# Two more products of a blocked matmul by an inner Strassen level, with one operand's block sums kept in DRAM

## The chip, the cores and the metric

The kernel runs on one core of a Trainium2 chip. The metric is the device time of one execution in microseconds (us): the median of nine runs, and beside it one execution taken by the hardware profiler, from which all durations come. TensorE (PE) multiplies, VectorE (DVE) and ScalarE (ACT) do elementwise work, GpSimd (POOL) small things, and SyncE (SP) issues nearly all DMAs from one queue.[...]

## The reference

```
x: 1 x 2048 x 1024 (bf16), w1: 1024 x 3584, b1: 3584, w2: 3584 x 1024, b2: 1024
y = (x - mean) / sqrt(var + 1e-5)          # per row of 1024
h = gelu(y @ w1 + b1)                      # tanh form
out = h @ w2 + b2
```

Matmul 1 is `y @ w1` with its bias and gelu, matmul 2 is `h @ w2 + b2`.

## The kernel before, in words

The 2048 rows are cut into two blocks of 1024 (`s` = 0 and 1). Each block runs matmul 1 and then matmul 2.

**Strassen (Winograd's form).** Each matmul of a block is split into 2 x 2 quarters and made of seven products in place of eight. A product multiplies a quarter or a sum of quarters (S1 to S4 on the side of the rows, T1 to T4 on the side of the weights), and the seven results are added up in PSUM and SBUF. In matmul 1 (`mm1_unit`, L579) this runs over seven chunks of w1 per block (numbered 0 to 6 in block 0 and 7 to 13 in block 1), two units in each; only chunk 0 is plain (`mm1_plain`). A unit is P1, P5, P6, P2, P7, P3, P4 (`SEQ1`), each four matmuls of 512 columns at L604, and the two units of a chunk alternate. ACT takes snapshots of PSUM (L617), DVE adds (L622, four per chunk) and ACT applies gelu (L628), which writes h in four quarters h11, h12, h21, h22, each of 14 slices of 128. DVE also forms T1 to T4 of each w1 chunk (L537).

**Matmul 2** (`mm2_block`, L746) has the order 5, 1, 2, 6, 7, 3, 4 (`SEQ2`). Products 5, 6 and 7 are plain (`plain`, L788): four tiles of 14 matmuls, 128 x 512, at L792. Products 1, 2, 3 and 4 (`INNER`) use a second, inner Strassen level (`inner`, L806): seven sub-products in the order of `SEQ1`, each 14 matmuls of 256 columns at L838. DVE forms the inner sums of both operands for each (four of h and four of w2, 128 x 1792, at L679): those of h into t1 buffers, those of w2 into old w1 buffers, and for the last product into others. Results are added up by ACT copies (L776) and DVE additions (L756), and stored from `o_sb` by SP (L785).

**The w2 operands.** Block 0's matmul 1 forms the outer sums T1 to T4 of w2 (`w2_prep`, L698) and writes them to DRAM (`w2_sums`). `load_w2` (L734) brings a whole quarter, raw or summed, 1792 KB in one DMA, into one of the homes A and B (`w2a_sb`), C (in `yw_sb`) and H (in `h_sb`). Block 1 loads seven such quarters.

**What sets the order.** Nothing is ordered by hand. Each operation is recorded with its dependencies, a cost and a due time, and a list planner (`Planner.place`, L127) fixes each engine's order and gives out PSUM banks and buffers. DMAs have a planned rate and a fixed time there. The program then has waits on semaphores in front of an instruction where its inputs come from another engine or a DMA; `war` lists name what must have finished before a buffer is written again. `done(p)` is the list of all users of product p, and `h_war` makes the gelus of the next block wait for the readers of a quarter of h.

**Block border.** While block 0's products 3 and 4 end, SP loads w1 for chunks 7 and 9 (chunk 8 is loaded long before), and T1 and B11 for block 1; the first units of block 1's matmul 1 are interleaved with product 4.

Of the kernel before, what the change touches and what calls it, by code (L numbers as in the profile page):

```python
# [6 lines left out]
ALU = mybir.AluOpType  # L7
BF16 = mybir.dt.bfloat16
# [23 lines left out]
SEQ2 = (5, 1, 2, 6, 7, 3, 4)  # L32
INNER = ((1, 2, 3, 4), (1, 2, 3, 4))
# [203 lines left out]
def bass_standalone__mixer_channel_mlp__prompt_kernel(  # L237
# [24 lines left out]
    with ExitStack() as es:  # L262
# [13 lines left out]
        e0_sb = sb("e0_sb", [P, HT // 2], F32)  # L276
        b1r_sb = sb("b1r_sb", [FT, P], BF16)
# [18 lines left out]
        NQ = NU * HT  # L296

# [6 lines left out]
        YN = KH * HT  # L304
        yop = {n: yw16[:, k * YN:(k + 1) * YN].rearrange("p (k n) -> p k n", n=HT)
# [357 lines left out]
        KI = NU // 2  # L663
        HI = HT // 2
# [29 lines left out]
        tq_ok = {r: [] for r in range(4)}  # L694
        x_gate = {}
# [50 lines left out]
        def mm2_block(s, W):  # L746
# [3 lines left out]
            for p in SEQ2:  # L750
                pt[p] = t0
                t0 += 7 * SUB if p in inn else TH * SLOT2
            A = {q: (h[q], [[h_ok[(s, q, u)]] for u in range(NU)]) for q in h}
            users = {p: [] for p in SEQ2}
# [26 lines left out]
            def store(q, t, n, ho, deps, at):  # L781
                r = (s * NT + (q // 10 - 1) * TH + t) * P
                c = (q % 10 - 1) * HT
                dst = of[r:r + n * P, c:c + HT].rearrange("(v p) c -> p v c", p=P)
                add("SP", 0.42, lambda e: e.dma_start(dst, o_sb[:, ho.k:ho.k + n, :]), deps, at + 0.5,  # L785
                    f"st{q}_{s}_{t}", sem=ho, inc=16, nbytes=n * P * HT * 2, frees=(ho,))
# [18 lines left out]

            def inner(p, a, b, xb, yb, war, O=None, bias=None, out=None, gate=()):  # L806

# [5 lines left out]
                Y = {f"{i + 1}{j + 1}": (b[0][:, i * KI:(i + 1) * KI, j * HI:(j + 1) * HI], b[1][i * KI:(i + 1) * KI])  # L813
                     for i in range(2) for j in range(2)}
                at = {r: pt[p] + k * SUB for k, r in enumerate(SEQ1)}

                def tt(dst, x, y, op, r, n):
                    return sums(dst, x, y, op, war.get((n[0], r), ()), at[r] - 3 * SUB, f"i{n}{r}_{nm}", step=KI)

                s1 = tt(xb[0], X["21"], X["22"], ALU.add, 5, "S")  # L820
                t1 = tt(yb[0], Y["12"], Y["11"], ALU.subtract, 5, "T")
                s2 = tt(xb[1], s1, X["11"], ALU.subtract, 6, "S")
                t2 = tt(yb[1], Y["22"], t1, ALU.subtract, 6, "T")
                s3 = tt(xb[2], X["11"], X["21"], ALU.subtract, 7, "S")
                t3 = tt(yb[2], Y["22"], Y["12"], ALU.subtract, 7, "T")
                s4 = tt(xb[3], X["12"], s2, ALU.subtract, 3, "S")
                t4 = tt(yb[3], Y["21"], t2, ALU.subtract, 4, "T")
                opn = {1: (X["11"], Y["11"]), 2: (X["12"], Y["21"]), 3: (s4, Y["22"]), 4: (X["22"], t4), 5: (s1, t1),
                       6: (s2, t2), 7: (s3, t3)}
# [23 lines left out]
                if O is None:  # L853
                    g = Holder(snaps, 4)
                    f1 = copy(lambda: bank_q(c2), lambda: bank_q(c0), (subs[1],), end(1), f"f1_{nm}", alloc=c2)
                    k5 = copy(lambda: quart(g, 1, 1), lambda: bank_q(c5), (subs[5],), end(5), f"k5_{nm}", alloc=g)
                    sub(6, (f1,))
                    k2 = copy(lambda: quart(g, 0, 1), lambda: bank_q(c0), (subs[6], k5), end(6), f"k2_{nm}")
                    sub(2, (f1,))
                    r11 = copy(lambda: quart(g, 0, 0), lambda: bank_q(c2), (subs[2], k5), end(2), f"r11_{nm}", frees=(c2,))  # L860
                    sub(7, (k2,))
                    r22 = dve(lambda e: plus(e, quart(g, 1, 1), bank_q(c0), quart(g, 1, 1)), (subs[7], k5), end(7),
                              f"r22_{nm}")
                    sub(3, (k5,))
                    r12 = dve(lambda e: plus(e, quart(g, 0, 1), bank_q(c5), quart(g, 0, 1)), (subs[3], k2), end(3),
                              f"r12_{nm}", frees=(c5,))
                    sub(4, (r22,))
                    r21 = copy(lambda: quart(g, 1, 0), lambda: bank_q(c0), (subs[4], k5), end(4), f"r21_{nm}", frees=(c0,))
                    users[p] += list(subs.values()) + flat(s1, s2, s3, s4, t1, t2, t3, t4)
                    return g, {11: r11, 12: r12, 21: r21, 22: r22}, subs  # L870

                g, ok = O
                ho = [Holder(outs, 2), Holder(outs, 2)]
                kk = Holder(snaps)

                def o_q(i, j):
                    return o_sb[:, ho[i].k:ho[i].k + 2, j * HI:(j + 1) * HI]

                sd = copy(lambda: bank_q(c2), lambda: quart(g, 0, 0), (ok[11], subs[1]), at[1], f"s2_{nm}", alloc=c2)
                k1 = copy(lambda: sn_sb[:, kk.k, :], lambda: ps[:, c0.k, :], (subs[1],), end(1), f"k1_{nm}", alloc=kk)  # L880
# [4 lines left out]
                o11 = dve(lambda e: plus(e, o_q(0, 0), bank_q(c2),  # L885
                                         sn_sb[:, kk.k, :].rearrange("p (v c) -> p v c", v=2)), (subs[2], k1), end(2),
                          f"o11_{nm}", alloc=ho[0], frees=(c2, kk))
# [6 lines left out]
                store(out, 0, 2, ho[0], (o11, o12), end(3))  # L894
                sub(4, (o22,))
                o21 = dve(lambda e: plus(e, o_q(1, 0), bank_q(c0), quart(g, 1, 0)), (subs[4], ok[21], o12, o22), end(4),
                          f"o21_{nm}", frees=(c0, g))
                store(out, 2, 2, ho[1], (o22, o21), end(4))
                users[p] += list(subs.values()) + flat(s1, s2, s3, s4, t1, t2, t3, t4)
# [13 lines left out]
            def war_of(subs):  # L913
                return {(c, r): [subs[r]] for c in "ST" for r in subs}

            B = dict(W)

# [12 lines left out]
            g1, ok1, sub1 = inner(1, A[11], B[1], X0, Y0, war0, gate=(M5[2],), bias=(  # L930
# [10 lines left out]
            sub2 = inner(2, A[12], B[2], X0, Y0, war_of(sub1), O=(g1, okw), out=11)  # L941
# [25 lines left out]
            sub3 = inner(3, S4, B[3], X0, Y0, war_of(sub2), O=(g12, {11: O12[1], 12: O12[1], 21: O12[3], 22: O12[3]}), out=12)  # L967
            for m in (n - 2, n):
                w1_use[m] = w1_use[m] + done(3)
            for m in (n - 1, n):  # L970
                for k in range(1, 5):
                    t1_use[m][k] = t1_use[m].get(k, []) + done(3)

            end_b = s + 1 == NSB
            xe = x16.rearrange("p i d -> p (i d)") if end_b else h_flat[21]
            inner(4, A[22], B[4], halves(xe), halves(w2a16[:, 1].rearrange("p k n -> p (k n)")),
                  {(c, r): [o for i in range(NT) for o in x_free[(s, i)]] if end_b and c == "S" else done(7)
                   for c in "ST" for r in range(1, 8)},
                  O=(g3, {11: O3[1], 12: O3[1], 21: O3[3], 22: O3[3]}), out=21)
# [3 lines left out]
            return {"A": done(3), "B": done(4), "C": done(2), "ring": ring}  # L983

        tile_prio = [-100 + 2.3 * i for i in range(NT)]
        for i in range(NT):
# [6 lines left out]
            else:  # L993
# [6 lines left out]
        bias_ok = add("DVE", 0.4, lambda e: e.tensor_tensor(out=e0_sb[:, :], in0=b2_sb[:, HI:HT], in1=b2_sb[:, 0:HI],  # L1000
                                                            op=ALU.subtract), (b2_ld, dl_), 60.1, "e0")
# [4 lines left out]
        for s in range(NSB):  # L1006
            last = []
            for c in range(NC):
                n = s * NC + c
                t0 = base1[s] + c * 14 * SLOT  # L1010
                if n:
                    T = w1_sums(s, c, t0 - 2 * SLOT)
                    for v in range(2):
                        last += mm1_unit(s, c, v, T, t0 + v * SLOT)
                m = n + N_W1
                if m < (s + 1) * NC:
                    load_w1(s, m % NC, t0 + 14 * SLOT)
                if s == 0 and c == 1:
                    gate = (w1_use[0][-1],)
                    t11 = load_w2(0, "B", "B11", gate, t0 + 0.1)  # L1020
                    t1q = w2_prep(t11[1][0][0], gate, t0 + 8, 8.5)
            if s == 0:
                W = {5: t1q, 1: t11}
            else:
                W = {5: load_w2(s, "A", "T1", wfree["A"], base1[s] + 0.3 * T_MM1),
                     1: load_w2(s, "B", "B11", wfree["B"], base1[s] + 0.3 * T_MM1 + 0.1)}
            W["C"] = last
            wfree = wf = mm2_block(s, W)
            if s + 1 < NSB:
                for c in range(N_W1):  # L1030
                    load_w1(s + 1, c, base2[s] + 40 + c)
                for i in range(NT):
                    load_x(s + 1, i, [*x_gate[i]], base2[s] - 4 + i)
                    ln_act2(s + 1, i, base2[s] + 10 + 5 * i, wf["ring"])
                    dma_T(s + 1, i, base2[s] + 30 + 3 * i, ((*last, *(wf["C"] if i >= TH else ())), last))
                y_sums(s + 1, base1[s + 1] - 14, wf["C"])
# [59 lines left out]
```

## Time and profile before

| | us |
|---|---|
| median of nine runs (lowest, highest) | 347.89 (346.82, 348.80) |
| profiled execution: device time, span | 347.71, 346.0 |
| head: 0 to 29.73 | PE busy 25.57 |
| matmul 1, block 0: 29.73 to 99.66 | PE 69.93, DVE 58.23, ACT 48.13, DMA 318 GB/s |
| matmul 2, block 0: 99.66 to 183.90 | PE 84.24, DVE 69.92, ACT 46.80, DMA 205 GB/s |
| matmul 1, block 1: 183.90 to 263.42 | PE 79.52, DVE 45.04, ACT 54.88, DMA 80 GB/s |
| matmul 2, block 1: 263.42 to 342.48 | PE 79.05, DVE 60.70, ACT 15.99, DMA 137 GB/s |
| tail: 342.48 to 346.00 | DVE 0.69, then the last store |

The granted TensorE clock is full in every slice. The whole run moves 63.01 MB by DMA. In the profile a row of a chain gives start, length and what ran; a row of an engine's timeline gives start, length, the instruction, and in brackets the idle time before it and what ended it. Matmul rows carry a length that includes the drain of the pipeline (a 256-column matmul has 273 ns there), so lengths per matmul are taken from the chain: stretch divided by count. SP's rows are issues; the time from issue to landing stands apart (10.6 us for the T1 load at the border, 3.8 to 6.8 for w1 halves).

### The profile page before, as it was taken

Reading aid. Unit: us, or ns where it says so; the run is one execution under the profiler, and the core shown is the slowest. Engines: PE = TensorE matmul, PEld = TensorE weight load, DVE = VectorE, ACT = ScalarE, POOL = GpSimd, SP = SyncE. Lnnn points to the kernel's source line nnn. Section 1 sums busy time; section 2 is a strip of 40 time slices with the busy share of each in tenths; the row PEclk is TensorE's granted clock in tenths of the full one; section 3 lists DMA queues with packets and bytes.
Section 4 is the critical chain, followed back from the end, with each engine's and each line's share of the span. In section 5 each row is a group of like instructions: output and inputs, shape, how many; then the busy total and the mean of one; then the engine's idle time right before and its main releaser. Section 6 shows DMA issues by size and latency. Waiting matters only on the chain.

```text
span 346.0 us, 5462 instructions
## 1 busy us (share of the span) xinstructions
PE 338.3 (98%) x2179; PEld 202.5 (59%) x2179; DVE 255.1 (74%) x356; ACT 183.5 (53%) x303; POOL 23.5 (7%) x47
## 2 busy tenths in 40 slices
PE   5999999999999999999999999999999999999995
PEld 4976444444444886448865444444444587644885
DVE  4679988989566698959999565465329779796943
ACT  4774766766788878622115767666676324002110
POOL 2320000000003223410000000000000000000000
PEclk9999999999999999999999999999999999999999
DMA  7649999988964792595398531230004256029111
GB/s 254 234 93 290 353 344 341 293 294 280 371 221 134 243 243 47 124 333 197 105 390 254 164 123 45 77 123 0 0 0 148 83 198 213 32 72 392 53 63 61
DMA packets 54339, 63.01 MB, mean 182 GB/s; under 512 B 12970, under 2 KB 47786, under 8 KB 53418
## 3 DMA queue, kind: packets, MB, share of 16 engines
q1 hardware_dynamic: 54170, 62.54, 55.9%
q8 instruction: 17, 0.28, 0.3%
q10 hardware_dynamic: 144, 0.13, 0.2%
q14 instruction: 8, 0.07, 0.1%
HBM read 48.50 MB, written 11.53 MB: 174 GB/s over the span
## 4 chain that ended last, share of the span: by engine, by line
PE 97%; DMA 1%; DVE 1%; ACT 0%; POOL 0%; issue 0%
PE ps L604 45%; PE ps L838 25%; PE ps L792 21%; PE ps L562 5%; PE ps L468 1%; DMA x_sb<-in_x_dram 1%; DVE st_sb L391 0%; DVE o_sb L756 0%; ACT yw_sb L475 0%; POOL rstd_sb L398 0%; DVE x_sb L401 0%; DVE mv_sb L394 0%; DVE vpe_sb L395 0%; PE ps L379 0%
## 5 line engine op out<-in xcount | busy, mean ns | idle before, releaser
L604 PE MATMUL ps<-yw_sb,t_sb 128*128 128x512 f16 x416 | 96.2, 379 | 0.0
L792 PE MATMUL ps<-w2a_sb,h_sb 128*128 128x512 f16 x336 | 73.8, 379 | 0.0
L604 PE MATMUL ps<-yw_sb,w_sb 128*128 128x512 f16 x312 | 73.7, 379 | 0.0
L604 PEld LDWEIGHTS ps<-yw_sb,t_sb 128*128 128x128 f16 x416 | 40.5, 98 | 48.9 <-ACT h_sb L628 0.4
L792 PEld LDWEIGHTS ps<-w2a_sb,h_sb 128*128 128x128 f16 x336 | 32.9, 98 | 38.3
L622 DVE TENSOR_TENSOR sn_sb<-ps,sn_sb 128x512 f32<-128x512 f32 x54 | 36.5, 687 | 25.5 <-PE ps L604 25.5
L604 PEld LDWEIGHTS ps<-yw_sb,w_sb 128*128 128x128 bf16 x312 | 30.3, 98 | 36.3 <-ACT ps L617 0.6
L628 ACT ACTIVATE h_sb<-sn_sb,b_sb 128x512 f16<-128x512 f32 x54 | 38.6, 719 | 19.1 <-DVE sn_sb L622 16.6
L776 ACT COPY sn_sb<-ps 128x512 f32<-128x512 f32 x30 | 17.2, 581 | 45.4 <-DVE o_sb L756 33.4
L679 DVE TENSOR_TENSOR h_sb<-h_sb 128x1024 f16<-128x1024 f16 (+2 forms) x42 | 38.5, 948 | 2.1 <-ACT h_sb L628 2.1
L628 ACT ACTIVATE h_sb<-ps,b_sb 128x512 f16<-128x512 f32 x50 | 34.1, 684 | 8.8 <-PE ps L604 7.9
L617 ACT COPY sn_sb<-ps 128x512 f32<-128x512 f32 x49 | 28.7, 586 | 16.0 <-PE ps L604 15.8
L756 DVE TENSOR_TENSOR o_sb<-ps,sn_sb 128x512 bf16<-128x512 f32 x32 | 21.7, 687 | 14.9 <-PE ps L838 10.9
L838 PE MATMUL ps<-w_sb,t_sb 128*128 128x256 f16 x252 | 30.1, 273 | 0.0
L838 PEld LDWEIGHTS ps<-w_sb,t_sb 128*128 128x128 f16 x252 | 24.7, 98 | 3.1
L537 DVE TENSOR_TENSOR t_sb<-w_sb,t_sb 128x1024 f16<-128x1024 bf16 x26 | 17.9, 687 | 8.3 <-PE ps L604 7.2
L838 PE MATMUL ps<-w2a_sb,h_sb 128*128 128x256 bf16 (+1 forms) x182 | 21.8, 273 | 0.0
L537 DVE TENSOR_TENSOR t_sb<-w_sb 128x1024 f16<-128x1024 bf16 x26 | 17.7, 681 | 5.2 <-PE ps L604 4.1
L776 ACT COPY ps<-sn_sb 128x512 f32<-128x512 f32 x14 | 8.1, 589 | 24.4 <-PE ps L838 20.6
L679 DVE TENSOR_TENSOR t_sb<-h_sb 128x1792 f16<-128x1792 f16 x12 | 13.0, 1085 | 9.6 <-PE ps L838 9.5
L838 PEld LDWEIGHTS ps<-w2a_sb,h_sb 128*128 128x128 f16 x182 | 17.8, 98 | 3.1
L756 DVE TENSOR_TENSOR sn_sb<-ps,sn_sb 128x512 f32<-128x512 f32 x24 | 16.4, 684 | 4.1 <-PE ps L838 2.6
(82 smaller groups left out, 321.5 us busy)
## 6 DMA issues: line engine op xcount, KB each, us to landing
w_sb<-in_w_dram SPq DMA_DIRECT2D x28, 512.0 KB, 5.4
w2a_sb<-w_sums SPq DMA_DIRECT2D x5, 1792.0 KB, 7.4
w2a_sb<-in_w_dram SPq DMA_DIRECT2D x4, 1792.0 KB, 7.4
x_sb<-in_w_dram SPq DMA_DIRECT2D x21, 256.0 KB, 4.6
w_sums<-x_sb SPq DMA_DIRECT2D x21, 256.0 KB, 4.9
x_sb<-in_x_dram SPq DMA_DIRECT2D x15, 256.0 KB, 5.4
yw_sb<-in_w_dram SPq DMA_DIRECT2D x2, 1792.0 KB, 7.5
h_sb<-w_sums SPq DMA_DIRECT2D x2, 1792.0 KB, 11.0
```

The source lines that it names most:

```text
L468: fn = [(lambda e, j=j, k=k, hold=hold: e.transpose(out=ps16[:, hold.k, j * P:(j + 1) * P], in_=x16[:, i, k * HT + j * P:k * HT + (j + 1) ...
L537: return add("DVE", 0.65, lambda e: e.tensor_tensor(out=tv(k), in0=x0, in1=x1, op=ALU.subtract), [*deps, *war.get(k, ())], prio + 0.5 * k, ...
L562: fn = [(lambda e, b=b, hb=hold[f], f=f, k=k, t=t: e.matmul(ps[:, hb.k, t * P:(t + 1) * P], lhsT=lhs[:, k, f * P:(f + 1) * P], rhs=yop[f"A ...
L604: fn = [(lambda e, k=k: e.matmul(ps[:, hold[p].k, :], lhsT=lhs[:, k, :], rhs=yop[yo][:, k, :], start=(first and k == 0), stop=(k == KH - 1 ...
L617: return e.copy(out=dst, in_=src) if o_.eng == "ACT" else e.tensor_copy(dst, src)
L622: return add("DVE", 0.69, lambda e: e.tensor_tensor(out=sn_sb[:, hold_s.k, :], in0=ps[:, hold[p].k, :], in1=sn_sb[:, hold_s.k, :], op=ALU. ...
L628: r = h_ok[(s, q, u)] = add("ACT", 0.70, lambda e: e.activation(out=h[q][:, u, :], in_=src(), func=ACT.Gelu_apprx_tanh, bias=b1_sb[:, f:f ...
L679: o = add("DVE", cost2(w * dst.shape[-1]), lambda e, k0=k0, k1=k1: e.tensor_tensor(out=dst[:, k0:k1, :], in0=a[0][:, k0:k1, :], in1=b[0][: ...
L756: plus = lambda e, out, x, y: e.tensor_tensor(out=out, in0=x, in1=y, op=ALU.add)
L776: return act(lambda e: e.copy(out=out(), in_=src()), deps, at, name, **k)
L792: fn = [(lambda e, k=k, t=t: e.matmul(ps[:, banks_[t].k, :], lhsT=a[0][:, k, t * P:(t + 1) * P], rhs=b[0][:, k, :], start=(first and k == ...
L838: fn = [(lambda e, k=k, j=j: e.matmul(ps[:, bank[r].k, j * HI:(j + 1) * HI], lhsT=x[0][:, k, j * P:(j + 1) * P], rhs=y[0][:, k, :], start= ...
```

## The change

In block 1, six of the seven products of matmul 2 are inner ones, only product 6 stays plain, and product 1 comes first. The w2 operands of an inner product come as seven separate blocks of 448 KB, four of them inner sums from a new DRAM tensor, three of them blocks of a quarter, in rows of 512 bytes. The inner sums of products 1 to 4 are the ones that block 0 forms anyway; it now also stores them. Those of T1 and T3, which products 5 and 7 need, are formed by DVE during matmul 1 of block 1, in buffers of x and of the outputs. Block 0's computation and order are kept otherwise. New waits: block 0's inner sums and everything that counts as done with a product also wait for the stores. The planner makes all orders anew.

The order of TensorE's instructions is the same up to the end of matmul 1 of block 1. In SP's new order, around the border, stand: a store of product 4's T2 sum, the four w1 halves, four blocks, an output store, the stores of product 4's T3 and T4 sums, two output stores, four blocks (after a wait for product 4's stores), the load of T1 for its inner sums (after a wait for all outputs of block 0), w1 loads, four stores of inner sums, the load of T3. On ACT, the first gelu of block 1 waits for product 4's inner stores and stands behind four snapshots. On DVE, the first inner sum of T1 stands between the second and third addition of chunk 8, and that of T3 behind the sum of h that follows chunk 9.

```diff
-SEQ2 = (5, 1, 2, 6, 7, 3, 4)
-INNER = ((1, 2, 3, 4), (1, 2, 3, 4))
+SEQ2 = ((5, 1, 2, 6, 7, 3, 4), (1, 5, 2, 6, 7, 3, 4))
+INNER = ((1, 2, 3, 4), (1, 5, 2, 7, 3, 4))
...
+        ti = nc.dram_tensor("w2_inner_sums", [7, 4, P, KI, HI], FP16, kind="Internal").ap()
...
+            def inner_sums(p, b, yb, war):
...
+                def tt(n, x, y, r):
+                    res = sums(yb[n - 1], x, y, ALU.subtract, war.get(("T", r), ()), at[r] - 3 * SUB, f"iT{r}_{nm}", step=KI)
+                    if s + 1 < NSB:
+                        st = dma(ti[p - 1, n - 1], yb[n - 1], res[1][0], at[r] + 1, f"is{p}_{n}", f"is{n}",
+                                 P * KI * HI * 2)
+                        ti_ok[(p, n)] = [st]
+                        users[p].append(st)
+                        ti_st.setdefault(p, {})[r] = st
+                    return res
...
-            def inner(p, a, b, xb, yb, war, O=None, bias=None, out=None, gate=()):
+            def inner(p, a, Yo, xb, war, O=None, bias=None, out=None, gate=(), kk=None):
...
+            def last_block():
...
+                def fetch(p, names, prio):
+                    res = {}
+                    for k, (r, b) in enumerate(zip(SEQ1, names)):
+                        d = blk[b]
+                        if r > 3:
+                            j = {5: 1, 6: 2, 7: 3, 4: 4}[r]
+                            o = dma(d, ti[p - 1, j - 1], [*use[b], *ti_ok[(p, j)]], prio + 0.1 * k, f"wi{p}_{r}",
+                                    f"wi{b}", P * KI * HI * 2)
+                        else:
...
+                            o = dma(d, src, [*use[b], *dep], prio + 0.1 * k, f"wi{p}_{r}", f"wi{b}", P * KI * HI * 2)
+                        res[r] = (d, [[o]] * KI)
+                    return res
...
+                hold = {1: ("A0", "A1", "A2", "A3", "B0", "B1", "B2"), 5: ("V0", "V1", "Y0", "Y1", "Y2", "Y3", "Y4"),
+                        2: ("W0", "W1", "Y5", "Y6", "Y7", "X0", "X1"), 7: ("B0", "B1", "B2", "B3", "V0", "V1", "Y0"),
+                        3: ("Y1", "Y2", "Y3", "Y4", "W0", "W1", "Y5"), 4: ("Y6", "Y7", "X0", "X1", "A0", "A1", "A2")}
+                Yo = {1: fetch(1, hold[1], base1[s] + 0.5 * T_MM1), 5: fetch(5, hold[5], pt[1] - 10),
+                      2: fetch(2, hold[2], pt[1])}
...
+                g1, ok1, sub1 = inner(1, A[11], Yo[1], XX, warE, gate=(jobs[-3],), bias=(
+                    b2_sb[:, None, 0:HI].to_broadcast([P, 2, HI]), e0_sb[:, None, :].to_broadcast([P, 2, HI])))
...
+                g5, ok5, sub5 = inner(5, S1, Yo[5], XT, warX, gate=(sub1[6],), bias=(
+                    dl_sb[:, None, 0:HI].to_broadcast([P, 2, HI]), e1_sb[:, None, :].to_broadcast([P, 2, HI])))
+                give(hold[5], sub5)
+                B6 = load_w2(s, "A", "T2", [o for k in range(4) for o in use[f"A{k}"]], pt[5])
...
+                    V.append(copy(lambda t=t: tile_of(gv, t), lambda t=t: bank_t(hb[t]), (M6[t], *V[:1]), at, f"V_{s}_{t}",
+                                  alloc=gv if t == 0 else None))
...
+                gw, okq, sub7 = inner(7, S3, Yo[7], XT, war_of(sub5), O=(gv, okv), kk=dl_sb[:, :], gate=(sub5[5],))
...
+                        f.append(dve(lambda e, i=i, j=j, ho=ho: plus(
+                            e, o_sb[:, ho.k:ho.k + 2, j * HI:(j + 1) * HI], quart(gw, i, j), quart(g5, i, j)),
...
+        def t_inner(p, j, gate, prio):
+            x4 = x16.rearrange("p i d -> p (i d)")[:, 0:NQ].rearrange("p (k n) -> p k n", n=HT)
+            ld = dma(x4, tq[j], [*gate, *tq_ok[j]], prio, f"tl{p}", "tl", NU * P * HT * 2)
...
+            a1, s1 = tt(1, ob[0], Y[0, 1], Y[0, 0], (ld, *gate))
+            a3, s3 = tt(3, ob[1], Y[1, 1], Y[0, 1], (ld, *gate))
+            a2, s2 = tt(2, Y[1, 1], Y[1, 1], ob[0], (a1, a3))
+            a4, s4 = tt(4, Y[1, 0], Y[1, 0], Y[1, 1], (a2,))
+            return [s1, s2, s3, s4, a4]
...
-                W = {5: load_w2(s, "A", "T1", wfree["A"], base1[s] + 0.3 * T_MM1),
-                     1: load_w2(s, "B", "B11", wfree["B"], base1[s] + 0.3 * T_MM1 + 0.1)}
+                x_end = [o for i in range(NT) for o in x_free[(s, i)]] + wfree["outs"]
+                e5 = t_inner(5, 0, x_end, base1[s] + 0.15 * T_MM1)
+                e7 = t_inner(7, 2, e5, base1[s] + 0.4 * T_MM1)
+                W = {"A": wfree["A"], "B": wfree["B"], "x": e7, "C": last}
```

## The prediction

> **What bounds the kernel now.** I read the busy rows first, then the chain that ended last, then busy time by stretch, then the queues at the one border that the change disturbs. The profile's busy rows and its shares of the chain:
>
> ```profile
> PE 338.3 (98%) x2179; PEld 202.5 (59%) x2179; DVE 255.1 (74%) x356; ACT 183.5 (53%) x303; POOL 23.5 (7%) x47
> PE 97%; DMA 1%; DVE 1%; ACT 0%; POOL 0%; issue 0%
> ```
>
> TensorE is busy 98% of the span, and the chain runs through it almost alone. The chain in order of time (start, length, what) has no gap from 29.73 us on; of block 1 it reads:
>
> ```profile
> 183.90 79.52 PE ps L604 x368
> 263.42 12.09 PE ps L792 x56
> 275.50 16.81 PE ps L838 x154
> ...
> 302.94 18.13 PE ps L792 x84
> 321.07 21.41 PE ps L838 x196
> 342.48 0.02 issue
> 342.50 0.69 DVE o_sb L756
> ```
>
> Each piece starts where the last one ends. So a matmul taken out anywhere in block 1 shortens the run by its own length, as long as no new wait replaces it; and a faster or slower DVE, ACT or queue changes nothing until TensorE waits for it. Two rows of busy time by stretch (length; PE, PEld, DVE, ACT, POOL; clock; DMA share; GB/s), an inner stretch and matmul 1 of block 1:
>
> ```profile
> 275.51:292.31 16.80, 16.80 (x155) 15.01 (x154) 13.22 (x15) 6.62 (x12) 0.00 (x0) 1.00 0.61 216
> 183.90:263.42 79.52, 79.52 (x369) 35.83 (x368) 45.04 (x68) 54.88 (x87) 0.00 (x0) 1.00 0.26 80
> ```
>
> The clock is full in both. Weight loads fill 15.01 of 16.80 us in the inner stretch and still hide. In matmul 1 of block 1 the DMA engines are three quarters idle and DVE has 34 us free: the room that the change means to use.
>
> **The change part by part.**
>
> *Products 5 and 7 of block 1 go inner.* From the chain, 56 matmuls of 512 columns take 12.09 us (215.9 ns each) and 154 of 256 columns 16.81 us (109.2 ns each). A plain product is 56 of the first, an inner one 7 x 14 = 98 of the second: 10.70 us. Two products: 2 x (12.09 - 10.70) = **2.78 us** off TensorE. The Trainium skill (TensorE: Matmul & The Clock Gate, "The mechanism") speaks against this: it says a weight load overlaps a running matmul only when it goes to another row group. Every load here is 128x128, so 98 ns would then stand bare before each matmul: inner 98 x (98 + 109) = 20.3 us against plain 56 x (98 + 216) = 17.6, and the change would lose 5.4. The stretch above refutes it for this kernel (15.01 us of loads inside 16.80 us of matmuls): I take the row.
>
> *Removed in block 1:* 16 sums of w2 blocks on DVE (1.08 us each, products 1 to 4). *Added on DVE:* 8 sums of h for products 5 and 7 and 8 w2 sums inside matmul 1, so none net; some 8 more additions of 512 (0.69 us) in the results of 5 and 7, about 5.5 us, in a block where DVE is busy 60.7 of 79.06 us. The four sums of two SBUF operands have no row; I take the 0.69 us of the additions from PSUM. The last of them frees the buffer that ACT's copy for product 3 takes at 320.4; it ends at 319.7, at twice the cost at 320.4. Cost nil while DVE stays within one sub-product (1.53 us) of TensorE, as it does now, and no gain either, since TensorE waits for neither today; each lost us would count in full. ACT gets four copies in product 6 and loses as many elsewhere; it has 16.0 us of work in 79.
>
> *Start of block 1.* It now begins with an inner product, whose second sub-product needs a sum over all of h11. The last gelu of h11 runs at 258.27 to 258.96; the sum (1.08) goes ahead of the chunk's four additions, done at 260.1. Its reader starts at 263.42 + 1.53 = 264.95. The additions behind it slip from 259.14 to 260.1, to be read by the fourth product at 261.5: cost nil, 0.7 us spare.
>
> *Blocks instead of quarters.* Six products fetch seven 448 KB blocks (0.459 MB) each in place of one 1.835 MB load: 3.21 MB per 10.70 us, so 0.30 MB/us is needed. The skill's page DMA: Bandwidth & Descriptors ("Measured") warns of this: 2.0 us fixed plus bytes/436 GB/s, best at 1 MiB or more. Seven blocks one after another would cost 7 x (2.0 + 1.05) = 21 us, twice the product that they feed. But the row for 29.73 to 99.66 us shows 256 KB pieces on the same queue at 318 GB/s: the fixed part overlaps. At that rate seven blocks take 10.1 us. Three of the seven come in 512-byte rows, which no row of the trace shows (its rows are 1 KB and more, at about 0.38 MB/us); I bound them between no penalty (1.2 us a block) and half rate (2.4), and take nearer the first. Even at half rate the first ten blocks after 263.4 us land by about 284, each before its sub-product (product 5 needs its third at 277.0, product 2 its third at 287.7), since buffers free one product ahead. SP waits in TensorE's own order there. Nil inside block 1.
>
> *Stores of inner sums in block 0* (16 x 0.459 MB). They stand in SP's queue between transposes and loads; the load of T3 and the second half of the transposes get waits for them. Product 1's last sum is stored behind a 1.835 MB load at 112.6 and lands near 121, T3 was issued at 122.48 and is needed at 148: nil. Transposes slip some 2 us and are needed at 162.55, landing near 160 now; they end by the same ACT work: nil, 2 us spare.
>
> *The border of the blocks* is where I expect trouble, if any. SP's queue of before there:
>
> ```profile
> 169.58 2.04 SPq L323 DMA_DIRECT2D w_sb<-in_w_dram  x4
> 171.66 0.53 SPq L323 DMA_DIRECT2D w2a_sb<-w_sums  x1
> 172.87 7.38 SPq L785 DMA_DIRECT2D out_dram<-o_sb  x2
> 183.93 0.38 SPq L323 DMA_DIRECT2D w2a_sb<-in_w_dram  x1
> 184.66 0.61 SPq L785 DMA_DIRECT2D out_dram<-o_sb  x1
> ```
>
> From the first of these to the w_sums load's landing (171.66 + 10.6) 4.19 MB moved in about 11 us: 0.38 MB/us. The changed queue, by its order: a T2 store ahead of the w1 loads, these (2.10), four blocks (1.84), an output store, the T3 and T4 stores of product 4; 5.57 MB from 170.5, so T4 lands near 185.2. Two things wait for that:
> - *ACT's first gelu of block 1*, since the h quarter counts as free only when product 4's stores have landed. Before it ran at 183.94; in the new order four snapshots (to 187.2) stand ahead of it. Behind it are eight activations of 0.62 us up to the next chunk's snapshots at 193.52, which leaves until 188.5 at no delay, and two more us by the snapshots' own readers. Nil.
> - *SP itself*, before four more blocks; behind it are the load of T1 for its inner sums, which also waits for the last output store (about 187.4), and w1 loads with 15 us to spare. Blocks and load are 4.2 MB with the stores, from 186.3: T1 lands near **197.5**; 202.3 if the 512-byte rows run at half rate.
>
> T1's first inner sum stands on DVE between the second and third addition of chunk 8:
>
> ```profile
> 199.57 0.69 DVE L622 TENSOR_TENSOR sn_sb<-ps,sn_sb 128x512 f32<-128x512 f32 x1 [0.17 <-PE ps L604]
> 200.17 0.68 DVE L537 TENSOR_TENSOR t_sb<-w_sb 128x1024 f16<-128x1024 bf16 x1
> 200.77 1.28 DVE L622 TENSOR_TENSOR sn_sb<-ps,sn_sb 128x512 f32<-128x512 f32 x2
> ```
>
> It is due at 200.2. If it waits, the two additions, two gelus and a bank copy queue behind it, about 3.7 us to the copy's end, which the third product of chunk 9 needs at 206.27. So TensorE waits only if T1 lands after **202.5**. T3's load follows the four inner stores (last sum near 205.6, landed 208 to 211), lands 215.5 to 218.5, and is due at 217.3 with the same kind of slack to 221. The first w1 half (landed 173.4) slips behind the T2 store (0.459 MB, 1.2 us) to about 174.6; chunk 7's P1 reads it from 174.83: nil to 1 us, I take nil. Together the border costs 0 to 1.5 us; I take 0.
>
> *Head and tail:* one more 256-wide sum near 60 us, hidden. The end is as before, last matmul, 0.69 us addition, store: 3.52 us.
>
> *Sum.* The profiled execution took 347.71 us, span 346.0 plus 1.7 around it; 347.71 - 2.78 = 344.93. It lies 0.18 below the median of 347.89, so for the median 347.89 - 2.78 = **345.1 us**, a span of 343.2. A measurement of this kernel tells some 0.2% (0.7 us) from no change.
>
> **The rivals.**
> - *All covers hold* (0.66): 345.1, own range 344.5 to 345.7. For it: no TensorE gap today, and every wait computed has slack.
> - *Part is lost at the border* (0.14): T1 at 203.5 or the w1 half late, about 1 us: 346.1, up to 347.2. For it: the 512-byte rows; 318 GB/s in the fullest stretch instead of 380.
> - *Given back* (0.08): stalls of 2.1 to 3.5 us, 347.2 to 348.6. That the change doesn't do what it says belongs here: sub-products that stand apart because block fetches come in their order too late.
> - *Slower* (0.12), one mechanism: DVE blocked on T1's load. 9.76 MB (5.57 + 4.19) and a pause of 1 us stand between 170.5 and its landing; it decides from a landing at 205.3 (0.29 MB/us) and exceeds 0.2% from 206. At 0.28 MB/us: 170.5 + 34.9 + 1 = 206.4, a stall of 3.9, so 349.0. For it: 257 GB/s at a DMA share of 0.83 in 139.2 to 157.3, beside transposes. Against: no transposes run at this border, and 0.38 was measured there.
>
> **How the numbers follow.** Likeliest is the first: 345.1. A range from 344.5 to 347.0 holds it and nearly all of the second. Faster: 0.66 + 0.14 = 0.80; same 0.08; slower 0.12.
>
> **What would show it.** Right: TensorE's busy time falls by 2.8 to 335.5, its chain in block 1 has no gap, 98 matmuls each for products 5 and 7, block 1's matmul 2 in 76.3 us instead of 79.06, T1's load landed before 202. Wrong: idle TensorE near 174, 188 to 195 or 200 to 221 with DVE or ACT waiting for a DMA; a gap ahead of a sub-product whose block is late; or 256-column matmuls above 109 ns because fetches disturb them.

## The result and the profile after

The changed kernel takes **344.7 us** (median of ten runs, 343.65 to 346.36), against 347.84 for the kernel before on the same chip; the ratio is 0.9916 with a 95% interval from 0.9901 to 0.9931. The forecast was 345.1. Its profiled execution took 344.89 us with a span of 343.2: 2.8 below the span before, as the sum said. The interval of the ratio stands for a gain of 2.4 to 3.4 us, so it means nothing that the medians lie 0.3 us further apart than the spans.

The busy rows of the changed kernel's page, and its shares of the chain:

```profile
PE 335.4 (98%) x2263; PEld 210.9 (61%) x2263; DVE 259.3 (76%) x363; ACT 184.3 (54%) x306; POOL 23.5 (7%) x47
PE 97%; DMA 1%; ACT 1%; SPq 0%; DVE 0%; issue 0%
```

TensorE has 84 matmuls more and is busy 2.9 us less; nothing else took its place in the chain. The chain in order of time (start, length, what) for block 1:

```profile
183.97 79.43 PE ps L608 x368
263.40 30.57 PE ps L864 x280
293.97 3.02 PE ps L797 x14
296.99 1.53 PE ps L864 x14
298.52 9.06 PE ps L797 x42
307.58 32.11 PE ps L864 x294
339.69 0.02 issue
339.71 0.69 DVE o_sb L761
```

Again each piece starts where the last ends. Of matmul 2, 588 short matmuls and the 56 long ones of product 6 are left: 339.69 - 263.40 = 76.29 us, where 79.06 stood. The 280 short ones at the start are 109.2 ns each (30.57 / 280), as before, beside far more DMA traffic. Busy time by stretch shows that traffic: matmul 1 of block 1, whose DMA share was 0.26, and matmul 2 (length; PE, PEld, DVE, ACT, POOL; clock; DMA share; GB/s):

```profile
183.90:263.42 79.52, 79.52 (x371) 36.07 (x370) 52.31 (x76) 54.55 (x88) 0.00 (x0) 1.00 0.62 210
263.42:339.70 76.28, 76.26 (x644) 62.76 (x642) 57.20 (x70) 17.23 (x31) 0.00 (x0) 1.00 0.68 225
```

At the border the new waits are there, and TensorE does not see them. The timeline of the changed kernel, ACT's first gelu of block 1 and DVE's first sums of T1 and T3 (in brackets the idle time before, and what ended it):

```profile
188.05 1.26 ACT L632 ACTIVATE h_sb<-ps,b_sb 128x512 f16<-128x512 f32 x2 [0.87 <-DMA w_inner_sums<-w2a_sb]
...
201.03 1.09 DVE L1138 TENSOR_TENSOR o_sb<-x_sb 128x1792 f16<-128x1792 f16 x1 [0.79 <-DMA x_sb<-w_sums]
...
220.29 2.09 DVE L1138 TENSOR_TENSOR o_sb<-x_sb 128x1792 f16<-128x1792 f16 x2 [3.04 <-DMA x_sb<-w_sums]
```

The three transfers that they wait for landed 2 to 5 us later than forecast, and each before the time from which it would cost something: 188.5, 202.5 and 221 by the prediction. That is close enough to ask whether those times are right, and whether the gain really is two shorter products and nothing else.

### The profile page after: what moved, and what is told of

Same layout as the page of the kernel before. It is cut to its first block, busy times and chain, and to the rows that moved or that the text cites. A ratio compares the mean times of both kernels' runs of the same rounds, so it can differ in the third digit from the quotient of the medians.

```text
span 343.2 us, 5750 instructions
## 1 busy us (share of the span) xinstructions
PE 335.4 (98%) x2263; PEld 210.9 (61%) x2263; DVE 259.3 (76%) x363; ACT 184.3 (54%) x306; POOL 23.5 (7%) x47
## 4 chain that ended last, share of the span: by engine, by line
PE 97%; DMA 1%; ACT 1%; SPq 0%; DVE 0%; issue 0%
PE ps L608 46%; PE ps L864 31%; PE ps L797 14%; PE ps L566 5%; DMA x_sb<-in_x_dram 1%; PE ps L472 1%; ACT h_sb L414 0%; SPq L327 0%; DVE o_sb L761 0%; ACT yw_sb L479 0%; ACT mv_sb L416 0%; PE ps L383 0%
## 5 line engine op out<-in xcount | busy, mean ns | idle before, releaser
L626 DVE TENSOR_TENSOR sn_sb<-ps,sn_sb 128x512 f32<-128x512 f32 x54 | 36.3, 687 | 18.6 <-PE ps L608 18.1
L797 PE MATMUL ps<-w2a_sb,h_sb 128*128 128x512 f16 x224 | 49.3, 379 | 0.0
L621 ACT COPY sn_sb<-ps 128x512 f32<-128x512 f32 x50 | 29.3, 586 | 19.9 <-PE ps L608 19.8
L797 PEld LDWEIGHTS ps<-w2a_sb,h_sb 128*128 128x128 f16 x224 | 21.9, 98 | 25.4
L781 ACT COPY sn_sb<-ps 128x512 f32<-128x512 f32 x30 | 17.3, 581 | 32.8 <-PE ps L797 19.4
L761 DVE TENSOR_TENSOR o_sb<-ps,sn_sb 128x512 bf16<-128x512 f32 x28 | 19.1, 687 | 13.7 <-PE ps L864 12.2
L761 DVE TENSOR_TENSOR sn_sb<-ps,sn_sb 128x512 f32<-128x512 f32 x31 | 21.3, 686 | 9.7 <-PE ps L864 9.0
L781 ACT COPY ps<-sn_sb 128x512 f32<-128x512 f32 x15 | 8.8, 589 | 34.5 <-PE ps L864 30.7
L864 PE MATMUL ps<-w2a_sb,h_sb 128*128 128x256 f16 (+1 forms) x196 | 23.5, 273 | 0.0
L864 PE MATMUL ps<-w_sb,t_sb 128*128 128x256 f16 x182 | 21.7, 273 | 0.0
L864 PEld LDWEIGHTS ps<-w2a_sb,h_sb 128*128 128x128 f16 x196 | 19.2, 98 | 3.3
L864 PEld LDWEIGHTS ps<-w_sb,t_sb 128*128 128x128 f16 x182 | 17.8, 98 | 2.3
L566 PE MATMUL ps<-yw_sb,w_sb 128*128 128x128 f16 x256 | 16.8, 230 | 0.4 <-ACT yw_sb L479 0.4
```

Source lines behind the costliest of these rows:

```text
L566: fn = [(lambda e, b=b, hb=hold[f], f=f, k=k, t=t: e.matmul(ps[:, hb.k, t * P:(t + 1) * P], lhsT=lhs[:, k, f * P:(f + 1) * P], rhs=yop[f"A ...
L621: return e.copy(out=dst, in_=src) if o_.eng == "ACT" else e.tensor_copy(dst, src)
L626: return add("DVE", 0.69, lambda e: e.tensor_tensor(out=sn_sb[:, hold_s.k, :], in0=ps[:, hold[p].k, :], in1=sn_sb[:, hold_s.k, :], op=ALU. ...
L761: plus = lambda e, out, x, y: e.tensor_tensor(out=out, in0=x, in1=y, op=ALU.add)
L781: return act(lambda e: e.copy(out=out(), in_=src()), deps, at, name, **k)
L797: fn = [(lambda e, k=k, t=t: e.matmul(ps[:, banks_[t].k, :], lhsT=a[0][:, k, t * P:(t + 1) * P], rhs=b[0][:, k, :], start=(first and k == ...
```

## The experiments

The theory: the gain is 1.39 us for each of two products on a TensorE without gaps, all the added work is hidden, and the border has a little over 1 us to spare before TensorE starts to wait. The rivals: part of the gain comes from elsewhere and pays for a cost at the border; or the late T1 load is not near any limit at all.

One thing is needed to read single profiles. The head ends at different times from run to run (first matmul of the long chain of block 0 at 29.81 in the changed kernel's profile, 28.77 to 30.64 in those below), which moves the span by up to 1 us. So I compare from that matmul to the end of the last one, **the body**: 312.75 us before the change (342.48 - 29.73), 309.88 after (339.69 - 29.81). The first two kernels with a dummy load, the one without the gelu's wait and the one with long rows ran once each, so what is said of them rests on one profile.

**Product 7 plain again.**

```
-INNER = ((1, 2, 3, 4), (1, 5, 2, 7, 3, 4))
+INNER = ((1, 2, 3, 4), (1, 5, 2, 3, 4))
...
-                Yo[7] = fetch(7, hold[7], pt[2])
+                B7 = load_w2(s, "B", "T3", [dead] + [o for k in range(4) for o in use[f"B{k}"]], pt[2])
...
+                M7 = plain(7, S3, B7, hb, False, [(o,) for o in O12])
```

(`dead` is the one block of product 7 that is fetched at the border; it is kept, unread, so that the queue stays as it was.)

> Product 7 of block 1 runs plain again; product 5 stays inner, and the sums of T3 are still formed and stored in matmul 1, so that the border is unchanged. Theory (the gain is nothing but shorter matmuls on a TensorE without gaps, 1.39 us a product): half of the gain goes, span 343.2 + 1.39 = 344.6, TensorE busy 1.4 more, median near 346.1. Rival A (the gain comes in part from the new order or from operands that lie ready as blocks, not from the inner level): the span stays below 344.3. Rival B (product 5 alone brings more or less than half, because each inner product saves a wait of its own): the span is off 344.6 by 0.3 or more.

Median 346.26, ratio to before 0.9957 (0.9941 to 0.9973), span 344.5; body 340.96 - 29.70 = 311.26, 1.38 more than after the change. The chain of this kernel from matmul 2 on:

```profile
263.29 32.10 PE ps L864 x294
295.38 24.17 PE ps L797 x112
319.55 21.41 PE ps L864 x196
```

Half of the gain is gone, with 112 long matmuls in place of 56. Rival A (a part from the new order or the blocks) and rival B (more or less than half) both fall.

**The preparations alone.**

```
-SEQ2 = ((5, 1, 2, 6, 7, 3, 4), (1, 5, 2, 6, 7, 3, 4))
-INNER = ((1, 2, 3, 4), (1, 5, 2, 7, 3, 4))
+SEQ2 = ((5, 1, 2, 6, 7, 3, 4), (5, 1, 2, 6, 7, 3, 4))
+INNER = ((1, 2, 3, 4), (1, 2, 3, 4))
...
-            if s + 1 == NSB:
-                last_block()
-                return None
...
+                W = {5: load_w2(s, "A", "T1", wfree["A"], base1[s] + 0.3 * T_MM1),
+                     1: load_w2(s, "B", "B11", wfree["B"], base1[s] + 0.3 * T_MM1 + 0.1), "x": e7, "C": last}
```

> All the preparations of the change are kept (block 0 stores its sixteen inner sums, the sums of T1 and T3 are formed in matmul 1 of block 1 and stored, with every wait of theirs), but block 1's matmul 2 is computed as before the change, in the old order. The stored sums are not read. Theory (all added work is hidden): span 346.0, as before the change, ratio to before 1.000. Rival (the border costs something that the gain covers up): span 346.3 to 347.5, with idle TensorE between 170 and 221 us.

Median 347.99, ratio to before 1.0008 (0.9990 to 1.0026), span 345.9, body 342.11 - 29.45 = 312.66: the time before the change to within 0.1 us. From its chain, the start of the body and its end:

```profile
29.45 69.93 PE ps L608 x324
...
183.61 79.43 PE ps L608 x368
...
320.70 21.41 PE ps L864 x196
```

Sixteen stores, two loads, eight sums and eight stores, with their waits, cost nothing that shows. They are hidden in this order of the queue, where T1's sum did not wait at all (DVE at 199.80 us); T3's waited 3.31 us here too. So this kernel does not try the border as the changed kernel has it; the next three do.

**A load in the way of T1's.** These three make the load of T1 late by a dummy load ahead of it, all orders kept.

```
+                n_ = 3
+                du = [dma(o_sb[:, 0:n_, :].bitcast(FP16), tq[j][:, 0:n_, :], [*gate, *tq_ok[j]], prio - 0.01, "du", "du", 1)]
             ld = dma(x4, tq[j], [*gate, *tq_ok[j]], prio, f"tl{p}", "tl", NU * P * HT * 2)
...
+        for ld, du in dummies:
+            ld.deps += du
```

The second and third have 7 in place of 3, and the last two lines, by which T1's load waits for the dummy, stand in the third alone.

> A load of 0.39 MB that nobody needs (into the buffer that T1's sums overwrite) stands in SP's queue just before T1's load at the border; orders are otherwise unchanged. At 0.32 MB/us it delays T1 by 1.2 us, to about 202.2 on DVE. Theory (TensorE waits only once DVE's first sum of T1 starts after 202.5): no stall by T1; the load of T3, which hangs on the stores of T1's sums, slips as much and had about 0.7 us to spare, so span 343.2 to 343.7. Rival A (no slack: each us of lateness counts): 344.4. Rival B (DVE's wait is harmless altogether): 343.2 here and in the next two.

> The same with 0.92 MB: T1 later by 2.4 to 2.9 us, to 203.4 to 203.9. Theory: TensorE waits 0.9 to 1.4 us near 206, and up to 2.2 in sum if T3 slips with it; span 344.1 to 345.4. Rival A (no slack): 345.6 to 346.1. Rival B (harmless): 343.2.

> The same 0.92 MB, and T1's load is issued only when it has landed, so that T1's sum starts near 206 to 207, about 5 us later than in the changed kernel. This is the mechanism of the prediction's slower case. Theory (a stall of one us for each us past 202.5): 3.5 to 4.5 us, span 346.7 to 347.7, no faster than before the change. Rival B (harmless): 343.2. Rival C (the additions behind the sum have more slack than was reckoned): a stall under 3 us.

In the first kernel the theory expected no stall, and there is one:

```profile
206.61 1.90 PE L608 MATMUL ps<-yw_sb,t_sb 128*128 128x512 f16 x8 [1.09 <-ACT ps L621]
```

Its span of 343.5 lies in the theory's range only because its head was 0.90 us shorter (28.91 in place of 29.81); the body lost 1.27 us. T1's sum came 2.30 us later, not 1.2. SP's rows show why (`o_sb` is the dummy, `x_sb` T1's load):

```profile
189.92 1.52 SPq L327 DMA_DIRECT2D o_sb<-w_sums  x1
191.48 0.65 SPq L327 DMA_DIRECT2D x_sb<-w_sums  x1
```

The issue of the dummy alone keeps SP for 1.52 us, and T1's load is issued 1.68 us later from the body's start than in the changed kernel. The bytes add only the other 0.6 us: T1's load takes 10.9 us to land in place of 10.3. In the second kernel it is 1.50 us by the issue and 1.07 by the bytes.

The third took 351.88 us, ratio 1.0117 to the kernel before (1.0079 to 1.0155): the slower case of the prediction, brought about by hand. DVE's timeline of the third kernel, at T1's first sum:

```profile
199.79 0.69 DVE L626 TENSOR_TENSOR sn_sb<-ps,sn_sb 128x512 f32<-128x512 f32 x1 [0.17 <-PE ps L608]
206.88 1.09 DVE L1144 TENSOR_TENSOR o_sb<-x_sb 128x1792 f16<-128x1792 f16 x1 [6.39 <-DMA x_sb<-w_sums]
207.89 1.28 DVE L626 TENSOR_TENSOR sn_sb<-ps,sn_sb 128x512 f32<-128x512 f32 x2
```

DVE stands 6.39 us before the sum, with the third and fourth addition queued behind it. TensorE's timeline there:

```profile
204.77 1.03 PE L608 MATMUL ps<-yw_sb,t_sb 128*128 128x512 f16 x4
208.63 1.04 PE L608 MATMUL ps<-yw_sb,t_sb 128*128 128x512 f16 x4 [2.83 <-DVE sn_sb L626]
211.05 3.33 PE L608 MATMUL ps<-yw_sb,t_sb 128*128 128x512 f16 x8 [1.39 <-ACT ps L621]
214.22 1.89 PE L608 MATMUL ps<-yw_sb,w_sb 128*128 128x512 f16 x8
```

The first wait ends with one of the additions, the second with ACT's copy into a bank: exactly the queue that the prediction names. The third row holds something else: eight matmuls take 3.33 us where the next eight take 1.89. The stretches of the same kernel say why (the column before the DMA share is the granted clock):

```profile
205.80:208.60 2.80, 0.00 (x0) 0.00 (x0) 1.72 (x3) 0.00 (x0) 0.00 (x0) 1.00 1.08 368
208.60:211.00 2.40, 1.04 (x4) 0.31 (x4) 2.37 (x3) 2.40 (x5) 0.00 (x0) 0.91 1.10 348
211.00:214.40 3.40, 3.35 (x9) 1.24 (x10) 3.26 (x6) 2.06 (x4) 0.00 (x0) 0.56 1.05 386
214.40:220.00 5.60, 5.60 (x27) 2.55 (x26) 5.16 (x10) 3.95 (x6) 0.00 (x0) 1.00 0.68 180
```

After 4.2 us of idle in two pieces the clock falls to half: it is 0.50 from about 210.6 to 214.0 us, and the 0.91 and 0.56 above are means of stretches that hold a part of that. TensorE's 264 matmuls up to matmul 2 take 58.58 us here and 57.15 in the second kernel: 1.43 us more on top of the wait. In the second kernel TensorE has one gap, and the clock stays full:

```profile
208.60 1.90 PE L608 MATMUL ps<-yw_sb,t_sb 128*128 128x512 f16 x8 [1.35 <-ACT ps L621]
```

Together, the start of T1's first sum counted from the start of the body, its slip against the changed kernel (171.22 us), and what the body lost:

| dummy | T1's sum, from the body's start | slip | body | lost | slip less loss |
|---|---|---|---|---|---|
| none | 171.22 | 0 | 309.88 | 0 | |
| 0.39 MB | 173.52 | 2.30 | 311.15 | 1.27 | 1.03 |
| 0.92 MB | 173.79 | 2.57 | 311.40 | 1.52 | 1.05 |
| 0.92 MB, waited for | 176.83 | 5.61 | 315.87 | 5.99, of it 1.43 slow clock | 1.05 |

Past the first 1.05 us each us of lateness costs one us. So TensorE begins to wait once T1's sum starts after 201.03 + 1.05 = **202.1** in the changed kernel's profile; the prediction had 202.5. Rival B (harmless) falls. So does A (no slack): its number for the first kernel, 1.2 us lost, is nearly met, but at a slip of 2.30 us it would have lost 2.30. C falls too: the slack is smaller than reckoned, not larger. The theory's rule holds, one us for each us past a limit; its numbers missed in the first kernel (no stall expected) and in the third (3.5 to 4.5 us expected, 5.99 lost, for it left the clock out). T3 added no wait: in the second kernel its sum starts at 223.39, which is 223.39 - 30.64 - 1.52 = 191.23 from the body's start with the stall taken out, 0.75 later than in the changed kernel (190.48), and TensorE has no gap there.

**No wait of the gelu for the stores.** The stores of product 4's sums read another buffer than the gelus write, so their wait can be dropped.

```
         order = pl.place()
+        for o in order["ACT"]:
+            o.deps = [d for d in o.deps if d not in ti_st[4].values()]
```

> The gelus of block 1 no longer wait for the stores of product 4's inner sums (which read another buffer than the one that gelu writes); orders are unchanged. Theory (that wait was hidden): the first gelu starts near 187.2, right behind the four snapshots, and the span stays 343.2, within 0.1. Rival (the wait took something that the gain covers up): the span falls by 0.2 to 0.8.

The first gelu starts at 186.83, right behind the snapshots, 0.86 us earlier from the body's start. The span is 342.9, but only because the head was 0.36 us shorter: the body is 339.44 - 29.45 = 309.99. So the wait cost nothing. (The extra 0.11 us lies in the sixteen matmuls of chunk 7 at 173.84, which take 3.57 in place of 3.45, ahead of any gelu of block 1. Its cause is not known.)

**Short rows replaced by long ones.**

```
-                            o = dma(d, src, [*use[b], *dep], prio + 0.1 * k, f"wi{p}_{r}", f"wi{b}", P * KI * HI * 2)
+                            src = ti[0, r - 1] if d.dtype == FP16 else ti[0, r - 1].bitcast(BF16)
+                            o = dma(d, src, [*use[b], *dep, *ti_ok[(1, r)]], prio + 0.1 * k, f"wi{p}_{r}", f"wi{b}", P * KI * HI * 2)
```

> Every block that comes in rows of 512 bytes is replaced by one of equal size in rows of 3584 bytes (a stored inner sum of product 1), so block 1 multiplies other data than it should; all else is as in the changed kernel. Theory (the short rows cost little, and what they cost is hidden): span 343.2 again, within 0.2; the T1 load lands at the border within 1 us of where it did, and DVE's first inner sum of T1 starts between 200.2 and 201.0. Rival (short rows run at about half rate and are what made T1 late): T1's sum no longer waits, starting at 200.24, and the fetches in matmul 2 move at a visibly higher rate than 342 GB/s; the span is still the same.

The body is 338.65 - 28.77 = 309.88, the same to 0.01 us (the span, 342.2, is lower by the head). The DMA rate is not the same. Two stretches at the start of matmul 2, first of the changed kernel, then of this one:

```profile
263.41:274.81 11.40, 11.40 (x107) 10.21 (x105) 10.66 (x13) 6.21 (x12) 0.00 (x0) 1.00 1.05 334
274.81:289.81 15.00, 15.00 (x140) 13.45 (x138) 10.93 (x13) 5.38 (x10) 0.00 (x0) 1.00 1.07 373
```

```profile
262.37:273.77 11.40, 11.40 (x106) 10.21 (x105) 10.67 (x13) 6.21 (x12) 0.00 (x0) 1.00 0.99 369
273.77:288.77 15.00, 15.00 (x140) 13.45 (x138) 10.93 (x13) 5.39 (x10) 0.00 (x0) 1.00 1.02 411
```

The engines are full in all four (share about 1), and long rows move 10% more (369 / 334 and 411 / 373): a cost far from half rate, hidden behind the matmuls. If all of it falls on the blocks in short rows, three in seven, one of these takes about a quarter longer (an estimate: 0.10 x 7 / 3). The blocks also come from another tensor in this kernel, so that row length and source are not told apart. At the border SP issues the block that waits for product 4's stores 0.85 us earlier from the body's start (at 186.19, against 188.08 in the changed kernel), T1's load 0.99 us earlier (188.67 against 190.70), and neither the gelu nor T1's sum waits. DVE's rows at T1's sum:

```profile
198.51 0.69 DVE L626 TENSOR_TENSOR sn_sb<-ps,sn_sb 128x512 f32<-128x512 f32 x1 [0.17 <-PE ps L608]
199.12 1.08 DVE L1139 TENSOR_TENSOR o_sb<-x_sb 128x1792 f16<-128x1792 f16 x1
```

T1's load takes 9.8 us and lands near 198.5, some 1.5 us earlier from the body's start; the theory had under 1 us and a sum that still waits. On these two signs, no wait and a visibly higher rate, the rival was right: with long rows T1 comes in time for its place on DVE. Its half rate is far off.

**Product 6 inner too.**

```
-INNER = ((1, 2, 3, 4), (1, 5, 2, 7, 3, 4))
+INNER = ((1, 2, 3, 4), (1, 5, 2, 6, 7, 3, 4))
...
-                B6 = load_w2(s, "A", "T2", [o for k in range(4) for o in use[f"A{k}"]], pt[5])
+                Yo[6] = fetch(6, hold[6], pt[5])
...
-                M6 = plain(6, S2, B6, hb, False, [(o,) for o in sdb])
+                gv, okv6, sub6 = inner(6, S2, Yo[6], XT, war_of(sub5), O=(gv, ok6), kk=dl_sb[:, :], gate=(kuse[2],))
...
+                e7 = t_inner(6, 1, e7, base1[s] + 0.6 * T_MM1)
```

> Product 6 of block 1 goes inner too, so that all seven are; T2's inner sums are formed in matmul 1 after those of T3, and ACT copies product 1's result for the second use. Theory: another 12.09 - 10.70 = 1.39 us, span 341.8, median near 343.3, if the covers hold: DVE gets four more sums in matmul 1 and some eight additions more in matmul 2, and the queue one load and four stores more near 235 to 250 us, where the DMA engines have room. Rival (DVE is now within one sub-product of TensorE in the last block and falls behind it): TensorE waits for DVE between 263 and 335 us and the span is 342.3 or more.

Median **343.34**, ratio to before 0.9879 (0.9855 to 0.9903), span 341.6, body 338.06 - 29.57 = 308.49: 1.39 less again. The end of this kernel's chain, and its stretches of matmul 1 and matmul 2 in block 1:

```profile
183.74 79.43 PE ps L608 x368
263.16 74.90 PE ps L865 x686
```

```profile
183.74:263.16 79.42, 79.42 (x370) 36.07 (x369) 55.94 (x79) 55.18 (x89) 0.00 (x0) 1.00 0.77 256
263.16:338.06 74.90, 74.89 (x687) 66.88 (x684) 64.96 (x80) 16.22 (x29) 0.00 (x0) 1.00 0.77 248
```

All of matmul 2 is one piece of 686 short matmuls at 109.2 ns. DVE, at 65 of 75 us, still keeps up. This version is the fastest of the kernels here.

## Why the prediction was right, point by point

- **Two products, 2.78 us.** Measured 2.77 in matmul 2 (79.06 to 76.29) and 2.87 in the body. The other 0.09 lie in matmul 1 of block 1 (79.52 to 79.43); the preparations alone have them too (79.43 in their chain), so they don't come from the two products. Why is open. Taking one product back cost 1.38, adding a third gave 1.39. The rule that a weight load to the same row group cannot overlap, which would have made the change lose 5.4 us, is again refuted: weight loads fill 66.88 of 74.89 us in the last kernel and matmuls keep their 109.2 ns. (The prediction quoted that section of the Trainium skill too narrowly: it also names a background weight buffer as a target of loads that are pulled ahead of running matmuls. That would fit these rows; no run here shows by which way the loads overlap.)
- **DVE, blocks, start of block 1, tail: nil.** TensorE's chain has no gap there. The additions of two SBUF operands took 0.69 us, the value taken from the PSUM ones. The formula set against the blocks, 2.0 us fixed plus bytes/436 GB/s, is given in the Trainium skill (DMA: Bandwidth & Descriptors, "Anatomy of one DMA — SWDGE (gpsimd) path") for a single DMA issued by GpSimd. From SP's queue the blocks came at 334 to 373 GB/s; one after another by that formula they would make 150 (an estimate: 0.459 MB in 3.05 us).
- **Stores in block 0: nil.** The preparations alone measure 1.0008.
- **The border: nil, but with 1.05 us left of a forecast 5.** This step named the right waits, the right queues behind them and nearly the right limit (202.5 against 202.1 measured). Its arrival times were wrong. The last store of product 4 landed at 188.05 where 185.2 was the forecast, so the gelu, forecast at 187.2 behind the snapshots, waited for it; T1 was there at 201.0, not 197.5; T3 at 220.3, not 215.5 to 218.5 (its load, which waits for the stores of T1's sums, was issued at 213.05; these were to land by 211). The mis-sized term is the rate for the whole way from start to landing: 0.38 MB/us was used, while 5.57 MB from 170.5 to 188.05 make 0.32. With 0.32 for the second part too, T1 comes out at 188.1 + 4.2 / 0.32 = 201.2, where it was.

  The reading behind 0.38 was loose. From the issue of the first row in that listing to the landing at 182.26 it is 12.7 us, not 11, which makes 4.19 / 12.7 = 0.33; 0.38 holds only from 171.2 us on, when the loads are moving. Full engines slowed down by 7% only: 388 GB/s before it (171.66 to 182.26), 361 after it (172.04 to 186.04), 379 in the kernel with long rows (171.0 to 185.0), which has the same stores among its loads; so these stores do not show as a lower rate. By the run with long rows, the short rows (or the tensor that they come from) account for 0.85 us of the 2.9 at the store and some 1.5 of the 3.5 at T1. Beside these, the engines are not full at the start (111 GB/s between 171 and 172 us), and the traffic stops near 187.3, 0.7 us before the landing shows; how the rest divides stays open. That "nil" came out with four fifths of its margin gone was in part luck.
- **The slower rival** was real in its mechanism and its place. At a start of 206.88 (206.64 counted as in the changed kernel) TensorE waited 4.56 us with the pipeline's drains (the rival had 3.9 for 206.4), and the clock added 1.43 that it didn't count. It did not occur because T1 came 1.05 us before the limit. "Every wait computed has slack" was true, with far less of it than reckoned.

## What to carry to other kernels

Where one engine's chain has no gap, the worth of a change on it can be counted in instructions of measured length, and then all the care belongs to the covers: write down for each new wait the time from which it costs, and compare it with an arrival reckoned at a rate that spans everything from the first issue to the last landing, not at that of engines already full. The late load at this border cost nothing up to its limit and one us per us beyond it, so a margin of 1 us in 345 deserves an experiment that uses it up. And compare profiles from a fixed instruction on, since the head alone moved the span by 1 us.

## What the runs showed of the hardware

- Two waits of 2.83 and 1.39 us on TensorE, with 1.0 us of work between them, were followed by some 3.4 us at a granted clock of 0.50; after a single wait of 1.35 us the clock stayed at 1.00. The Trainium skill (TensorE: Matmul & The Clock Gate, "Part 1: The HAM clock gate (the "warmup" mystery)") says that the clock falls to half after an idle window of about 3.4 us. The half rate agrees; but no wait here was as long as that, and TensorE had worked 1.0 of the 3.4 us before the clock fell. In this run the stall cost a third more than its wait (5.99 against 4.56 us).
- Each gap also cost 0.17 us beyond the idle time shown (0.39 MB: 1.27 lost, 1.09 shown; 0.92 MB: 1.52 and 1.35). That is about the 0.16 us by which the row of a matmul is longer than its place in the chain (273 ns against 109).
- Blocks of 448 KB with three in seven in rows of 512 bytes moved 9% less per us, with the DMA engines full, than the same number all in rows of 3584 bytes from another tensor (373 against 411 GB/s).
